# Loading q and k by tiles of all heads, and turning the last batch's q and k in the DMA path, in a fused attention and gated-convolution kernel

## The chip, the cores and the metric

The kernel runs on one core of a Trainium2 chip. The metric is device time in microseconds (us) of one execution. The core has five queues of instructions, each of which runs its own in order: PE (matrix products, with weight loads shown apart as PEld), DVE (vector), ACT (scalar), POOL (GpSimd) and SP (which here only issues transfers). Transfers run on 16 DMA engines. POOL's loads (the software queue) can change float32 to float16 on the way; SP's (the hardware queue) can't.

## What is computed

Four batches, eight heads, 768 positions, 64 numbers per head. First an attention in which each position sees the 95 positions before it, itself, and the first 8 positions of the sequence, with a bias that grows with distance by a slope of each head; then a gated convolution over the sequence on the joined heads (512 columns).

```python
scores = scale * q @ k.T                       # per batch and head, 768 x 768
keep = (pos_k < 8) | ((0 <= rel) & (rel < 96))  # rel = pos_q - pos_k
scores = where(keep, scores - slope[h] * dist, -1e9)
x = softmax(scores) @ v                        # heads joined: (4, 768, 512)
x1, x2, x3 = split(x @ w_proj)                 # 3 x 512 columns
conv = irfft(rfft(x2) * rfft(filter))          # circular, along the sequence
out = (x1 * conv * x3) @ w_out
```

## The kernel before

**Tiles.** Keys are cut into seven tiles: 120 local keys each (`KL`, starts in `K0`; the last overlaps the sixth) below the 8 global ones. A key tile meets a window of at most 216 queries (`EW`). The seven tiles form three groups, `GRP = (0,1), (2,3), (4,5,6)`; the eight heads form four pairs, and a head pair's 128 numbers fill the partitions of `QT` and `KT`, the turned q and k. Both are there once, as are `qn` and `kn`, the float16 rows before turning, and `E`, the exponentials; `vn` is there twice.

**A batch's attention** (`attention`, L849). For each head pair `turned` (L623) turns q and k on PE (six 128 x 128 transposes into one PSUM bank, L629) and ACT or DVE copies the bank out: one copy for q (L632), three for k (L635: five sixths of the tiles, the last tile, the 8 global columns for all seven). Then per group and head pair `scores` (L645: products L663, the exponential on ACT L674, the mask on DVE L691); `values` (L694: products L709 and L714, reciprocal and scaling L738, L733 or L737), `transpose_x` (L743), `gate` (L822: x1 and x3, products L832, L838, L846), and `butterfly` (L761), which folds the sequence for the short transforms. In batch 0 the bias enters by a product (L657) instead of the mask.

**A batch's convolution** (`conv`, L876): the projection of x2 (L890), its spectrum (L999), products with the filter's spectrum, the inverse (L914, L917), `mixed` and `gated` on DVE, then the output product (L946), its copy (L311) and the store on SP (L952).

**Loads.** In batch 0 q and k of head pairs 0 and 1 (`PLAIN`) come through SP as float32 into borrowed buffers (`h1`, `h2`, `pp`) and are cast by DVE (`load_pair`, L339). All else comes through POOL: q and k one head at a time (768 rows of 256 bytes, L344), v by tiles of 120 rows of all heads (960 rows, L329), weights, and the filter. `distances` (L507) makes the table of distances on POOL (L516 to L523: two iotas and four selections) and a second table (L539).

**What sets the order.** `graph` (L1084) lists the operations with their numbers. `ORDER` (L41) is one list, written out, of these numbers, each with the engine that runs it (P, A, V, G, S) and the PSUM banks that it takes; words such as `i3b6` are three dummy products on PE. Each engine's queue holds its part of this list in that order; semaphores are set only where data demand it. `bias`, costs and `after` served the making of the list; `after` also holds the list to that order, and sets no semaphore by itself.

Of the kernel before, what the change touches and what calls it, by code (L numbers as in the profile page):

```python
# [17 lines left out]
P = 128  # L18
NG = 8
KL = P - NG  # L20
# [21 lines left out]
0V 1V 2A 49S 11V 3G 5V 4V 7G 9V i3b6 17P0 46V 44A 18A 12P1 19V 55G 51S 56G 20V 43A 54G 13A 45A 42A 50V 22P2  # L42
47A 38V 14V 15V 23A 32S 52V 10V 41V 16A 53G 77G 24V 36G 90P3 39G i1b6 92P1 61S 60G i3b6 96P0 59G 48V 25V 58G
57G 30V 91A 67G 33V i4b6 86P2 93A 37V 65G 62A 21A 40V 94P1 26A 66G 104P45 87A 97V 34S 122P23 78A 63V 95V
106P01 29V 105A 68G 6V 35V 107A 156P67 88P4 8V 157A 31V 69G 89V 123A 124P01 120P45 70G 214V 215V 71G 102P67
100P2 121A 74G 158P45 216V 103A 125A 249G 98P3 101V 154P67 159A 99V 64S 235G 155A 108P23 126P45 110P67 217V
250G 160P01 218V 109A 127A 219V 111V 220V 112V 238G 161A 247G 75G 248G 115P23 128P45 133P67 227P0 113P1 116V
72G 83A 117V 134V 85A 129V 241G 225P2 237G 135V 118P3 162P67 130V 167P45 73G 114V 131P1 27A 228A 226A 81A 28V
80A 206P2 163V 223P0 164V 132A 168V 136P1 236G 165P6 240G 169V 221P7 119V 166V 84A 170P3 189V 245G 246G 137A
209V 82A 242G 224A 79A 146P6 150P1 152A 171V 229P45 239G 352P3 151P1 222A 188V 244G 243G 197V 213A 211A 76G  # L50
191V 353A 350P7 147P0 251G 231V 180P5 148V 184P3 198V 351A 153V 230A 149V 385P01 199V 190V 182A 363P67 200V
207V 476G 201V 386A 475G 364A 142P4 138P5 186A 340P0 259G 254G 338P1 232P67 212A 341A 192V 144V 193V 202V 233A
194V 387V 339V 143P3 210A 203V 185P4 140A 176P6 256G 252S 354P01 208A 145V 423P23 234A 187V 178V 196V 414P45
355A 415A 255G 344P7 342P6 195V 139P0 348P1 345V 257G 343V 424A 356V 365V 204V 141V 181P7 474G 349A 379P23
473G 357P45 346P6 347V 461G 462G 258G 472G 172P1 183V 177P0 358A 484G 376P45 417P67 380A 359V 174A 360P23 205V
179V 377A 274P1 425V 261P0 253S 418A 361A 381V 420P67 382P45 416V 362V 265P2 421A 383A 469G 275A 263P3 471G
264A 371P45 378V 419V 422V 366P67 384V 289P1 372V 367V 262A 173P3 373V 466G 287P0 266A 388P45 368V 175V 290A
389V 288A 291V 374P2 269P6 267P7 369P3 375A 270A 268A 278P0 276P2 370A 463G 279A 577P3 393P01 390V 277A 280P2
292V 578A 271V 575P7 272V 470G 394V 576A 426P45 273V 465G 281A 282P3 477G 283A 391P6 395V 431P01 396P7 392A
397A 701G 427V 588P23 480G 428V 301P4 432V 285V 433V 589A 429P5 468G 464G 284V 410P7 430A 467G 573P6 434P0  # L60
482G 610P23 406P5 302A 571P4 706G 590V 574A 611A 305P6 699G 435V 306A 286V 695G 297P0 298A 303P1 412A 572V
295P2 453V 293P4 299P3 452V 296A 307P6 481G 308A 694G 294A 304A 300V 485G 563P0 398P7 698G 402P6 585P23 408A
400A 455V 567P1 404A 310V 309V 607P45 407P7 586A 691G 454V 686G 311V 564A 568A 608A 403P6 569P2 411P3 405V
570A 440P6 399P1 456V 565P0 442A 312V 457V 582P45 409V 696G 478S 609V 458V 401V 566A 645P67 646A 693G 583A
436P2 459V 413V 499P0 639P67 640A 486P1 313V 692G 500A 479S 437P3 697G 460V 314V 438A 487A 587V 601P67 604P45
501P2 690G 483G 439V 444P3 315V 612V 602A 687G 605A 579P67 647V 648P01 709G 446A 502A 603V 448P4 642P23 580A
643A 584V 606V 688G 445P5 794P6 618P23 649A 641V 792P7 795A 447V 596P01 793A 644V 581V 597V 700G 450A 619V
503P5 504A 796P6 788P7 598V 613P01 620V 316V 591P23 800P5 614V 260G 689G 514P4 789A 449P7 797A 507P6 592V 615V
651P01 515A 801A 508A 593V 505P2 650V 317V 867P45 318V 506A 594P3 798P6 451V 868A 490P2 799A 595A 656P45 319V
657V 652V 802P7 488P6 491A 658V 803A 616P2 441P3 599P7 659P4 489A 617A 621P6 510V 492P5 653V 509V 600A 512P2  # L70
622A 443V 493A 511V 654P7 494P0 513A 320P6 495A 635P5 707G 321A 813P01 329P2 516V 496V 655A 660A 702G 870P67
869V 814A 637A 330A 636P4 517V 335P0 807P23 677V 638V 678V 871A 497V 808A 832P45 673P1 679V 790P6 520P7 680V
703S 627P2 833A 681V 532P3 704S 521A 632P7 815V 675A 873P45 631P1 533A 682V 791A 332P6 498V 874A 526P3 524P4
708G 629A 705G 633A 522P2 527A 525A 333A 518P1 674P5 834V 683V 875V 685V 336A 322S 523A 628P4 710G 530P6 531A
528P0 676V 684V 634V 519A 630V 323P5 835P23 809V 810P67 529A 804P01 726P4 324A 811A 836A 864P67 711P5 623P2
805A 535V 334S 331S 865A 534V 812V 715P3 536V 826P67 829P01 625A 712A 806V 537V 716A 713P5 830A 821P23 827A
837V 538V 872V 326P0 816P67 727A 737P4 539V 714A 822V 540V 823V 724P1 817V 327A 543V 818A 669P0 866V 541V
843P23 844V 738A 671A 828V 725A 728P5 717P4 729A 730P6 845V 665P7 718A 731A 831V 542V 719P1 739P0 624P5 720A
838P23 626V 740A 667A 670P6 325S 839V 840A 732P0 881P45 722V 672V 544V 876P67 733A 741V 819P1 661P2 662P0 877V
882V 878V 820A 721V 337S 560P1 883A 879P3 824P6 663A 735V 666P7 723V 884P4 548P2 825A 841P6 846P5 885A 742V  # L80
668V 734V 880A 664V 755P4 842A 736V 847A 747P3 557P7 756A 753P6 757P0 902V 751P4 328S 748A 903V 743P3 754A
749P5 758A 752A 905V 750A 745P6 746A 848P0 904V 744A 759V 545P4 852P3 554P6 906V 854A 911P3 546A 924P4 912A
760V 907V 551P3 549A 937P2 925A 850A 761V 908V 762V 849P4 939P0 909V 938A 910V 763V 561A 913P2 547S 851V 555A
764V 562S 940A 558A 914A 857P1 928P0 929A 917P2 915P7 918A 926P0 916A 919P2 927A 941V 920A 853P7 552A 765V
942V 930P0 932P6 766V 860P2 931A 768V 767V 550S 933A 922V 856P3 770P0 921V 858A 935V 553S 556S 923V 934V 773P3
771A 943P0 962P6 862A 774A 947P2 944A 948A 855V 936V 861P4 769V 963A 958P0 945P5 949P2 959A 964P3 863V 946A
950A 960P6 772S 776P0 779P2 965A 961A 859V 775S 777A 951V 952V 780A 967V 966V 953V 968V 785P6 954V 782P7 969V
559S 955V 890P2 898P3 970V 956V 778S 900A 971V 781S 887P0 957V 972V 894P1 886P3 973V 783A 892A 975V 974V 786A
976V 988V 896V 899P2 986V 977P6 978A 895P7 888A 983P1 897V 984A 784S 901V 787S 891P7 889V 980P6 981A 893V 979S
989V 985S 987V 999P6 993P7 1000A 982S 994A 1001S 995S 996P6 997V 990P0 998S 991A 992S  # L90
# [108 lines left out]
class Fused:  # L199
# [7 lines left out]
    LATE = frozenset(())  # L207
# [27 lines left out]
    def buffers(self):  # L235
# [5 lines left out]
        self.qn = t("qn", [P, 4, 6, 2, D])  # L241
        self.kn = t("kn", [P, 4, 6, 2, D])
# [32 lines left out]
        self.under = [[("h", 0), ("h", 2)], [("h", 1), ("h", 3)]] + [[(x, i) for x in ("p1", "p2") for i in range(2)]] * 2  # L275
        self.y = t("y", [P, 4, S])
# [43 lines left out]
    def load(self, eng, dst, src, w, nbytes, name, r=()):  # L320
        self.loads += 1
        e = {"G": self.nc.gpsimd, "S": self.nc.sync}[eng]
        return self.g.op(eng, 0.57 + 0.00035 * nbytes[0] if eng == "G" else 0.5, lambda _: e.dma_start(dst, src),  # L323
                         w=w, r=r, nbytes=nbytes, name=name, bias=-2000.0 + self.loads)
# [8 lines left out]
    def load_run(self, what, dst, src, t, n):  # L333

        rows = src[0, :, self.K0[t]:self.K0[t] + KL * n, :].rearrange("h (t p) d -> p t h d", t=n)
        self.load("G", dst[NG:P, t:t + n, :, 0:self.D], rows, [what + (i,) for i in range(t, t + n)],
                  (8 * KL * n, 256), f"load{what}{t}")

    def load_pair(self, b, hp):  # L339
        for i, (what, x, dst) in enumerate((("q", self.q, self.qn), ("k", self.k, self.kn))):  # L340
            to = dst[:, hp]
            if b or hp not in self.PLAIN:
                for hh in range(2):
                    self.load("G", to[:, :, hh], x[b, 2 * hp + hh].rearrange("(t p) d -> p t d", p=P),  # L344
                              [(what + "n", hp, hh)], (768, 256), f"{what}{hp}")
# [3 lines left out]
            self.load("S", st, x[b, 2 * hp:2 * hp + 2].rearrange("h (t p) d -> p (h t) d", p=P),  # L349
                      own[0:1], (1536, 256), f"{what}{hp}")  # L350
            st = st.rearrange("p (h t) d -> p t h d", h=2)
# [16 lines left out]
    def load_w(self, o, n):  # L368
        wr = self.w_proj.rearrange("(t p) n -> p t n", p=P)
        self.load("G", self.w[:, :, o:o + n], wr[:, :, o:o + n],  # L370
                  [("w", i) for i in range(o // P, (o + n) // P)], (512, 4 * n), f"w{o}")
# [791 lines left out]
```

## Time and profile before

| what | us |
|---|---|
| median of 3 runs (lowest, highest) | 172.21 (170.92, 172.63) |
| the profiled execution, as timed | 171.85 |
| its span in the profile | 170.1 |
| POOL's last load issue ends | 87.0 |
| turning of q and k on PE, first and last start | 5.3, 102.1 |
| score products (L663), first and last start | 12.2, 114.2 |
| first store to the output issued by SP | 97.8 |
| last product on PE ends | 166.3 |

The span begins with the first instruction and ends with the last; 1.75 us of the timed execution lie outside it. Busy times of matrix products are modelled, since they overlap one another, so a PE that is busy throughout need not run at its peak. "Landing" is the time from the issue of a transfer to the first sign that it arrived. The order's 1006 words stand for 1002 operations and 4 groups of dummy products.

### The profile page before, as it was taken

To read this page: it belongs to the slowest core of one execution; us is meant where nothing else is said; L and a number is where in the kernel's file an instruction comes from. 1 tells how busy PE (TensorE), PEld (TensorE's weight loads), DVE (VectorE), ACT (ScalarE), POOL (GpSimd) and SP (SyncE) were. 2 spreads that over 40 slices of the span, in tenths; PEclk is the share of its full clock that TensorE was granted. 3 is DMA by queue.
4 is the path that set the end of the run, shared out by engine and by line. 5 is a ranking of instruction groups with operands and counts; after the bars stand their busy time and mean duration, and the time that the engine had idled before them with its cause. 6 is when DMAs were issued, how large, how long until landed. Compare 5 with 4: busy or idle time off the path is not lost. (4 is left out here: it accounts for less than half of the span.)

```text
span 170.1 us, 4259 instructions
## 1 busy us (share of the span) xinstructions
PE 160.6 (94%) x1614; PEld 96.2 (57%) x1614; DVE 155.9 (92%) x364; ACT 150.2 (88%) x308; POOL 81.9 (48%) x107
## 2 busy tenths in 40 slices
PE   7795998999999999999999999999999999999981
PEld 2452347766655688555677546646577644565540
DVE  5993789999999999999999999999999999999950
ACT  5779499999999999999999999999999789894441
POOL 8997999999799899999940000000000000000000
PEclk9999599999999999999999999999999999999999
DMA  6999999999999999999999110330100013343344
GB/s 133 194 200 190 154 158 166 176 160 161 157 158 136 130 111 135 121 133 112 135 148 91 14 62 4 123 123 14 51 2 4 0 62 123 129 185 123 149 186 158
DMA packets 87139, 20.30 MB, mean 119 GB/s; under 512 B 79872, under 2 KB 84176, under 8 KB 87120
## 3 DMA queue, kind: packets, MB, share of 16 engines
q0 software_dynamic: 76976, 11.84, 95.5%
q1 hardware_dynamic: 10144, 8.20, 15.6%
q8 instruction: 12, 0.20, 0.5%
q14 instruction: 7, 0.06, 0.1%
HBM read 25.25 MB, written 6.29 MB: 185 GB/s over the span
## 5 line engine op out<-in xcount | busy, mean ns | idle before, releaser
L832 PE MATMUL bank<-xT,w 128*128 128x384 f16 x256 | 49.1, 326 | 0.0
L674 ACT ACTIVATE E<-bank 128x864 f16<-128x864 f32 x48 | 41.8, 952 | 2.5 <-PE bank L663 2.5
L832 PEld LDWEIGHTS <-w 128*128 128x128 f16 x256 | 23.5, 98 | 16.3 <-issue 1.1
L323 POOL DMA_DIRECT2D vn<-in_v_dram x28 | 26.1, 959 | 2.5 <-DMA g<-in_moe_filter_fft_dram 1.4
L323 POOL DMA_DIRECT2D kn<-in_k_dram x28 | 24.0, 869 | 0.8 <-PE bank L629 0.7
L946 PE MATMUL bank<-wo,y 128*128 128x512 f16 (+1 forms) x100 | 23.7, 370 | 0.7 <-DVE y L995 0.7
L323 POOL DMA_DIRECT2D qn<-in_q_dram x28 | 23.8, 864 | 0.3 <-PE bank L917 0.2
L691 DVE TENSOR_TENSOR E<-E,mask 128x864 f16<-128x864 f16 x36 | 20.4, 595 | 0.0
L311 ACT ACTIVATE ot<-bank 128x512 f32<-128x512 f32 (+1 forms) x24 | 14.9, 636 | 5.4 <-PE bank L946 4.8
L311 ACT ACTIVATE x<-bank 128x384 f16<-128x384 f32 x28 | 15.8, 590 | 3.6 <-PE bank L832 3.4
L846 DVE TENSOR_TENSOR g<-bank,x 128x384 f16<-128x384 f32 x32 | 17.0, 547 | 0.5 <-ACT X L307 0.3
L733 DVE TENSOR_TENSOR xn<-bank,rc 128x512 f16<-128x512 f32 (+1 forms) x21 | 15.9, 771 | 0.1
L890 PE MATMUL bank<-w,xs 128*128 128x512 f16 x64 | 16.0, 379 | 0.0
L709 PE MATMUL bank<-vn,E 128*128 128x65 f16 x224 | 15.2, 193 | 0.7 <-DVE xn L733 0.5
L663 PE MATMUL bank<-QT,KT 64*128 64x216 f16 (+2 forms) x224 | 15.6, 248 | 0.0
L714 PE MATMUL bank<-vn,E 128*128 128x65 f16 x192 | 15.0, 193 | 0.0
L946 PEld LDWEIGHTS <-y 128*128 128x128 f16 x100 | 9.5, 98 | 9.6 <-DVE y L995 1.2
L709 PEld LDWEIGHTS <-E 128*128 128x128 f16 x224 | 13.9, 97 | 1.5 <-issue 0.3
L307 ACT CAST X<-bank 128x512 f16<-128x512 f32 x24 | 14.7, 732 | 0.0
L663 PEld LDWEIGHTS <-KT 64*128 64x128 f16 x224 | 7.8, 95 | 12.0 <-issue 10.8
L714 PEld LDWEIGHTS <-E 128*128 128x128 f16 x192 | 13.2, 97 | 1.7 <-issue 1.1
L307 ACT COPY KT<-bank 128x720 f16<-128x720 f16 (+2 forms) x36 | 13.6, 524 | 0.2 <-PE bank L629 0.2
(156 smaller groups left out, 343.6 us busy)
## 6 DMA issues: line engine op xcount, KB each, us to landing
out_dram<-ot SPq DMA_DIRECT2D x23, 256.0 KB, 2.0
vn<-in_v_dram POOLq DMA_DIRECT2D x28, 120.0 KB, 6.3
kn<-in_k_dram POOLq DMA_DIRECT2D x28, 96.0 KB, 5.2
qn<-in_q_dram POOLq DMA_DIRECT2D x28, 96.0 KB, 4.9
w<-in_moe_w_proj_dram POOLq DMA_DIRECT2D x4, 256.0 KB, 6.4
g<-in_moe_filter_fft_dram POOLq DMA_DIRECT2D x1, 768.0 KB, 11.3
w<-in_moe_w_proj_dram POOLq DMA_DIRECT2D x1, 512.0 KB, 7.4
wo<-in_moe_w_out_dram POOLq DMA_DIRECT2D x1, 512.0 KB, 8.1
```

Of the source, the lines that this page charges most:

```text
L307: {"A": nc.scalar.copy, "V": nc.vector.tensor_copy, "G": nc.gpsimd.tensor_copy}[e](out, in_)
L311: self.nc.scalar.mul(out, in_, c)
L323: return self.g.op(eng, 0.57 + 0.00035 * nbytes[0] if eng == "G" else 0.5, lambda _: e.dma_start(dst, src), w=w, r=r, nbytes=nbytes, name= ...
L663: nc.tensor.matmul(bs[hh].f32()[:, off:off + w], self.KT[hs, hp, P * m:P * m + P], self.QT[hs, hp, KL * m:KL * m + w], start=(off == 0 and ...
L674: g.op("A", act(864), lambda _: nc.scalar.activation(eo, bs[0].two()[:, :, 0:432].rearrange("p h (m w) -> p h m w", m=2), Act.Exp, scale=s ...
L691: g.op("V", dve(864, 2), lambda _: nc.vector.tensor_mul(eo, eo, mk), r=[("mask", 2 * hp), ("mask", 2 * hp + 1)], w=[("E", hp, gi)], name=" ...
L709: nc.tensor.matmul(o[:, n, hh], ef[:, at:at + P], vt[:, t, 2 * hp + hh, 0:D + 1], start=first, stop=(t == 0), skip_group_check=True)
L714: nc.tensor.matmul(o[:, n, hh], ef[:, at:at + P], vt[:, t - 1, 2 * hp + hh, 0:D + 1], start=False, stop=True, skip_group_check=True)
L832: nc.tensor.matmul(bk.f32()[:, 0:h], self.w[:, c, o + P * j:o + P * j + P], self.xT[:, c, h * s:h * s + h], start=(c == 0), stop=(c == 3))
L846: g.op("V", dve(h, 1, True), lambda _: nc.vector.tensor_mul(x3, pts[1].f32()[:, 0:h], x1), use=[pts[1]], r=[key], w=[ko], name="g")
L890: nc.tensor.matmul(bk.f32(), src[:, c], w[:, c, DM:2 * DM], start=(c == 0), stop=(c == 3))
L946: nc.tensor.matmul(bk.f32()[:, 0:n], y[:, c, P * t:P * t + P], self.wo[:, c, cs], start=(c == 0), stop=(c == 3))
```

## The change

Four things change, and `ORDER` is a new list of 994 words (990 operations, 4 groups of dummy products).

- **q and k of batches 1 to 3 by tiles.** `qn` and `kn` lie by tile, `[P, 6, 512]` and `[P, 7, 512]`. `load_tiles` replaces eight loads each of 768 rows by six each of 128 rows of all heads (1024 packets). The six transposes of a head pair read all six tiles; a tile can be overwritten when all four head pairs are turned.
- **The last batch (`CROSS = (3,)`) is not turned on PE.** Its keys are loaded as seven tiles of 120 rows, the 8 global rows are copied within SBUF into the first partitions (two transfers on SP), and `cross` issues 13 transposing transfers on SP, each turning a tile `[128 rows, 512]` into `[128, 4, 128]` of `KT` or `QT`. The 8 operations of `turned` and their 8 copies go. The score products of that batch wait for tiles of `KT` and `QT` instead of head pairs.
- **POOL's start.** The first table of distances stands ahead of POOL's first loads.
- **The order.** The engines of the copies that ACT or DVE can make are chosen anew, too. In the new list SP's first loads are k of pair 1, q of pair 0, v's first rows, q of pair 1, k of pair 0 (before: q1, k1, q0, v's first rows, k0), and POOL's are the filter, then single heads of k and q of pairs 2 and 3.

The counts of operations by engine in the two lists, where they differ:

| operation | before | after |
|---|---|---|
| loads of q, k, v by POOL | 84 | 73 |
| turns on PE | 32 | 24 |
| copies of turned q: ACT, DVE | 10, 6 | 5, 7 |
| copies of turned k: ACT, DVE | 12, 4 | 8, 4 |
| scaling of values (two tiles): ACT, DVE | 2, 14 | 6, 10 |
| copies of turned x (two tiles): ACT, DVE | 14, 2 | 10, 6 |
| same, three tiles: ACT, DVE | 5, 3 | 6, 2 |
| casts of batch 0's q, k: ACT, DVE | 0, 4 | 3, 1 |
| copies of x1: ACT, DVE | 28, 4 | 30, 2 |
| outputs: ACT, DVE | 24, 1 | 21, 4 |
| scaling of the projection: ACT, DVE | 24, 0 | 22, 2 |
| transposing transfers on SP | 0 | 13 |

```diff
-    LATE = frozenset(())
+    CROSS = (3,)
...
-        self.qn = t("qn", [P, 4, 6, 2, D])
-        self.kn = t("kn", [P, 4, 6, 2, D])
+        self.qn = t("qn", [P, 6, DM])
+        self.kn = t("kn", [P, 7, DM])
...
+    def load_tiles(self, b):
+        sides = [("q", self.q, self.qn, P, 0, range(0, self.S, P)), ("k", self.k, self.kn, P, 0, range(0, self.S, P))]
+        if b in self.CROSS:
+            sides[1] = ("k", self.k, self.kn, KL, NG, self.K0)
+        for n in range(7):
+            for what, x, dst, rows, low, starts in sides:
+                if n < len(starts):
+                    lo = starts[n]
+                    self.load("G", dst[low:P, n].rearrange("p (h d) -> p h d", h=self.H),
+                              x[b, :, lo:lo + rows, :].rearrange("h p d -> p h d"),
+                              [(what + "n", n, h) for h in range(8)], (8 * rows, 256), f"{what}{n}")
+            if n == 0 and b in self.CROSS:
+                for lo, hi in ((0, 2), (2, 7)):
+                    self.load("S", self.kn[0:NG, lo:hi], self.kn[NG:2 * NG, 0:1].to_broadcast([NG, hi - lo, self.DM]),
+                              [("kg", lo)], (8 * (hi - lo), 1024), "vglobal", r=[("kn", 0, h) for h in range(8)],
+                              after=self.turns)
+
+    def cross(self):
...
+                out = dst[:, :, P * n:P * n + P]
+                self.g.op("S", 1.3, lambda _, out=out, src=src, n=n: nc.sync.dma_start_transpose(out, src[:, n]),
...
+                          w=[(what + "T", n)], nbytes=(128, 1024), name="xbar",
+                          after=loads + [x for gi in gis for x in self.before[gi]])
...
-                nc.tensor.transpose(b.f16()[:, P * t:P * t + P], buf[:, hp, t].rearrange("p h d -> p (h d)"), self.ident)
+                nc.tensor.transpose(b.f16()[:, P * t:P * t + P], buf[:, t, P * hp:P * hp + P], self.ident)
...
+        src = [("QT", hp), ("KT", hp)]
+        if self.b in self.CROSS:
+            src = [("kT", m) for m in m0] + [("qT", n) for n in range(KL * m0[0] // P, (
+                KL * m0[-1] + self.EW[m0[-1]] - 1) // P + 1)]
...
-            if c == 0:
+            if c == 0 and b in self.CROSS:
+                self.cross()
+            elif c == 0:
...
+        self.distances()
         for i in range(4):
-            self.load_pair(0, i)
-            if i == 0:
-                self.distances()
+            self.load_pair(i)
...
-        for i in range(4):
-            self.load_pair(b, i)
+        self.load_tiles(b)
```

More of the change, by code (lines that the diff above doesn't have):

```diff
@@ L47 @@
[L47 to L51, printed above, removed]
@@ L317, in evac, with load @@
         return {"A": act(n), "V": dve(n, psum=True)}
-    def load(self, eng, dst, src, w, nbytes, name, r=()):
+    def load(self, eng, dst, src, w, nbytes, name, r=(), after=()):
         self.loads += 1
@@ L323, in load @@
         return self.g.op(eng, 0.57 + 0.00035 * nbytes[0] if eng == "G" else 0.5, lambda _: e.dma_start(dst, src),
-                         w=w, r=r, nbytes=nbytes, name=name, bias=-2000.0 + self.loads)
+                         w=w, r=r, nbytes=nbytes, name=name, after=after, bias=-2000.0 + self.loads)
     def load_rows(self, what, dst, src, b, t):
@@ L352, in load_pair @@
             self.g.op("AV", {"A": act(768), "V": dve(768, 2)}, lambda e, to=to, st=st: self.copy(e, to, st),
-                      r=own, w=[(what + "n", hp, 0), (what + "n", hp, 1)], name="cast")
+                      r=own, w=keys[0] + keys[1], name="cast")
+    def load_tiles(self, b):
[14 more added lines that the diff above has]
+                              after=self.turns)
@@ new lines, in cross @@
+    def cross(self):
+        nc, S = self.nc, self.S
+        loads = [x for x in self.g.ops if "G" in x.cost and x.bytes]
+        for n in range(7):
+            for what, src, dst, ok in (("k", self.kn, self.KT, True), ("q", self.qn, self.QT, n < 6)):
+                if not ok:
+                    continue
+                gis = [gi for gi, ms in enumerate(self.GRP) if (n in ms if what == "k" else any(
+                    KL * m < P * n + P and KL * m + self.EW[m] > P * n for m in ms))]
+                out = dst[:, :, P * n:P * n + P]
+                self.g.op("S", 1.3, lambda _, out=out, src=src, n=n: nc.sync.dma_start_transpose(out, src[:, n]),
+                          r=[(what + "n", n, h) for h in range(8)] + ([("kg", 0 if n < 2 else 2)] if what == "k" else []),
+                          w=[(what + "T", n)], nbytes=(128, 1024), name="xbar",
+                          after=loads + [x for gi in gis for x in self.before[gi]])
@@ L370, in load_w @@
         self.load("G", self.w[:, :, o:o + n], wr[:, :, o:o + n],
-                  [("w", i) for i in range(o // P, (o + n) // P)], (512, 4 * n), f"w{o}")
+                  [("w", i) for i in range(o // P, (o + n) // P)], (512, 4 * n), f"w{o}", after=self.ahead)
     def setup(self):
@@ L628, in turn @@
             for t in range(6):
-                nc.tensor.transpose(b.f16()[:, P * t:P * t + P], buf[:, hp, t].rearrange("p h d -> p (h d)"), self.ident)
-        g.op("P", pe(*[P] * 6), turn, acq=[b], r=["ident", (what + "n", hp, 0), (what + "n", hp, 1)], name=what)
+                nc.tensor.transpose(b.f16()[:, P * t:P * t + P], buf[:, t, P * hp:P * hp + P], self.ident)
+        self.turns.append(g.op("P", pe(*[P] * 6), turn, acq=[b], r=["ident"] + [
+            (what + "n", t, 2 * hp + hh) for t in range(6) for hh in range(2)], name=what))
         if what == "q":
@@ L1063, in load_first @@
         self.load("G", self.fl, self.filt.rearrange("(t p) n -> p t n", p=P),
-                  [("g", 1, j, s) for j in range(4) for s in range(2)], (768, 2048), "filter")
+                  [("g", 1, j, s) for j in range(4) for s in range(2)], (768, 2048), "filter", after=self.ahead)
     def first_rows(self, vt):
```

118 lines of the change are left out of this document (64 added, 54 removed).

## The prediction

> **What bounds the kernel now.** I read the busy times first, then the stretches of time, then the by-shape groups of the operations that go, then the start on DVE, SP and POOL.
>
> ```profile
> PE 160.6 (94%) x1614; PEld 96.2 (57%) x1614; DVE 155.9 (92%) x364; ACT 150.2 (88%) x308; POOL 81.9 (48%) x107
> ```
>
> Three engines are nearly full. The stretches (columns: length, then busy time of PE, PEld, DVE, ACT, POOL, the granted clock, DMA share, GB/s) say where they aren't:
>
> ```profile
> 15.00:20.00 5.00, 3.25 (x20) 1.04 (x20) 3.86 (x11) 3.18 (x5) 3.55 (x5) 0.75 2.26 160
> 30.00:40.00 10.00, 10.00 (x110) 6.70 (x106) 9.78 (x26) 9.67 (x20) 9.75 (x13) 1.00 2.06 163
> 100.00:110.00 10.00, 10.00 (x100) 6.29 (x98) 9.97 (x21) 10.00 (x23) 0.00 (x0) 1.00 0.14 52
> 150.00:160.00 10.00, 10.00 (x70) 5.83 (x69) 10.00 (x30) 5.96 (x15) 0.00 (x0) 1.00 0.46 176
> ```
>
> From 30 to 160 us PE and DVE run at 98% or more, ACT nearly so until 130. What is idle lies at the start (DVE 6.3 us, ACT 6.4 us in the first 30) and in the last 8 us. So the time can fall in two ways: less work on all three engines, or an earlier filling. What goes is shown by the by-shape groups (busy us, mean ns, idle before):
>
> ```profile
> L307 ACT COPY KT<-bank 128x720 f16<-128x720 f16 x12 | 10.3, 857 | 0.2 <-PE bank L629 0.2
> L629 PE MATMUL bank<-ident,kn 128*128 128x128 f16 x96 | 8.8, 233 | 2.5 <-DVE kn L307 2.5
> L307 ACT COPY QT<-bank 128x768 f16<-128x768 f16 x10 | 8.5, 906 | 0.4 <-PE bank L629 0.4
> ```
>
> The start, from the timelines of DVE and SP (start, length, operation, idle before it and what ended that):
>
> ```profile
> 16.00 0.56 DVE L307 CAST kn<-h 128x768 f16<-128x768 f32 x1 [2.25 <-DMA h<-in_k_dram]
> 5.41 0.39 SPq L323 DMA_DIRECT2D h<-in_k_dram  x1
> ```
>
> The fifth SP load, k of pair 0, is issued at 5.41 and arrives at 16.0. PE waits 1.7 us for it, ACT then 1.8, and the clock in the stretch falls to 0.75. In the window 3 to 5 us, with POOL's packets not yet there, SP's queue had the DMA engines to itself:
>
> ```profile
> q1 hardware_dynamic: 1943, 0.49, 130.3%
> q0 software_dynamic: 21, 0.00, 2.1%
> ```
>
> That is 1.03 ns a packet; later, mixed with POOL's packets, it moved 0.36 MB in 4 us.
>
> **The change, part by part.** *Turns on PE.* 48 of 192 transposes go. Six of them take 0.50 us in PE's timeline and one alone 0.22, so their pitch is 0.057 us: 48 x 0.057 = 2.7 us. They lie among PE's full stretches, so it counts if PE is the one that ends last.
>
> *Copies on ACT and DVE.* By the two orders' letters and the rows' busy time over count: on ACT four k copies of 1.57 (10.3 + 4.5 + 4.0 over 12) and five q copies of 0.85 go, 10.5 us; with four two-tile x copies of 0.63, three outputs of 0.63 and two projections of 0.72, 16.3. Back come four scalings of values (eight small activations of 0.24 each, 7.7 us), three casts of some 0.85, two x1 of 0.56 and 0.8 of single ones, 12.1. Net -4.2 us. On DVE scalings (4 x 0.66), casts (3 x 0.59), x1 (2 x 0.55) and single ones (1.7) go, 7.2; x copies (4 x 0.40), outputs (3 x 0.68), projections (2 x 0.68), a q copy and small ones (1.2) come, 6.2. Net -1.0 us.
> With all three engines full the saving is at least DVE's 1.0, if DVE ends last everywhere, and at most PE's 2.7. I take 1.9, the middle, since waits between 30 and 160 us change sides too often for one engine to own them.
>
> *POOL's first loads behind the distances.* The table takes 2.3 us (6.44 to 8.78) and now stands before the loads, which start at about 4.4 instead of 2.06; the same set of issues is done by about 13 us either way. The packets of the first POOL load came 3 us after its issue, so SP has the engines alone until about 7.3: from 1.85 us at 0.25 to 0.28 MB/us, its 1.59 MB are through by 8 to 9. So k of pair 0 comes at about 9 instead of 16. Upper end of the gain: DVE's 2.25 us and 1.2 behind it, 3.4. Lower end: what comes next. The new PE queue turns all four k of batch 1, does four x1 gates and turns q before it goes on, and with tiles a turn needs the last of six loads.
>
> *Tile loads.* 768 packets take POOL 0.87 us, 960 take 0.96, so 0.48 ns more a row and 0.99 for 1024. Twelve of these are 11.9 against 16 x 0.87 = 13.9: 2.0 us less for batches 1 and 2 each, 1.2 for batch 3, whose seven k tiles carry 576 packets more. POOL is idle after 87 us, so by itself this is worth nothing; it brings the last load to about 80, landing (5 to 6 us) by 86. But q of batch 1 is now complete only when POOL, past batch 0's v at 20.8 as before, has issued 12 tiles and a weight load: 20.8 + 12.7 = 33.5, and 5.2 to land, 38.7. PE was at its first gate at 33.2; four k turns (1.4), a filter product (0.4) and four gates (2.8) bring it to 37.8, less what the start gained. It would wait for whatever is gained beyond -0.9. So the start is worth between -0.9 and 3.4; I take 0.5, near the lower end, since this wait is counted from rows and the engines behind it have work left.
>
> *The crossbar.* 13 transfers on SP, of 128 KB each, and two small copies. No row shows a transposing transfer. Below: q's load at 1.03 ns per 256 bytes is 0.53 us for 512 such packets. Next: SP spaced its loads of 384 KB by 1.6 to 1.7 us. Above: if the crossbar works in 32-byte pieces, 4096 x 1.03 = 4.2 us. I take 1.5, near the spacing row, as that is the same queue under load. The sources: the turns of batch 2 free `qn` at about 66 us (by the place in the order: products of batch 2's scores ran from 62 to 82); 14 loads of about 0.96 later POOL is at 80, q lands by 85. The score products of batch 3 stand in the new order where the old one was at 103 to 116 us; the last group needs all 13 tiles at about 113. Twelve after 85 with 2 us to land may take (113 - 85 - 2) / 12 = 2.2 us each; the first group's five have more. So at 1.5 it is hidden with 8 us to spare. Behind it on SP wait the stores, first due at 97.8 before; six output buffers cover them. If the cover is gone, PE, ACT and DVE wait in order: PE's queue holds the projections of batch 2 behind those products.
>
> A rule speaks against this part. The Trainium skill (VectorE: DVE Perf Modes, "The three transpose paths") gives 1309 ns for one 128 x 128 turn in the DMA crossbar against 390 on TensorE, and says to use TensorE where PSUM will do. Here PE's pitch is 57 ns, far below that page's figure; whether its 1309 holds for each of the four squares of a transfer no run shows. By an estimate from it, four in a row make 5.2 us a transfer, and the sum would be some 205 us; from rows this is the first rival.
>
> *Sum.* -1.9 - 0.5 = -2.4 us on 171.85; the median is 0.36 above the profiled run, so 172.2 - 2.4 = 169.8. Best case, -2.7 - 3.4: 166.1.
>
> **Rivals.** *Slow crossbar, slower.* It decides from 2.2 us a transfer. At 3 us: 85 + 36 + 2 = 123 against 113, ten late: 169.8 + 10 = 180. At 4.2: 85 + 50 + 2 = 137: 194. For it: nothing in the trace bounds the piece size. Against: the loads are over by then, and the DMA share is 0.14 between 100 and 110 us. Chance 0.19.
> *Late tiles.* Turns wait for the slowest of six loads, in batch 1 as above and again in batch 2, whose q tiles are reissued only after all four q turns. The start's gain is lost (-0.9) and 0.5 to 1 us goes at batch 2: 172.2 - 1.9 + 0.9 + 0.8 = 172.0, up to 175 if both engines behind run dry. For it: POOL is 98% busy from 30 to 80, so a tile can't be pulled in. Against: DVE and ACT have other work queued. Chance 0.29, of which 0.05 over 1% slower.
> *Not behind all loads.* `after` sets no semaphore, so transposes could run beside the last loads, as k of pair 0 did at 10.6 us. But the second transposing transfer needs the last q tile but one, so only one overlaps; it costs nothing and belongs to the forecast.
>
> **How the numbers follow.** A measurement of this kernel can tell about 1% (170.5 to 173.9) from no change. Forecast, 166.1 to 170.4: 0.52. Late tiles: 0.24 within 1%, 0.05 above. Slow crossbar: 0.19. So faster 0.52, same 0.24, slower 0.24. The range for 8 in 10 runs from 166.1 to 177, which leaves out the slow crossbar above 2.7 us a transfer (0.15) and a little below.
>
> **What would show it.** Right: the cast of k of pair 0 before 11 us, no fall of the clock before 20; PE's turns 144; the transposing transfers spaced under 2.2 us and over before 110; ACT's busy time about 146, DVE's 155. Wrong: PE idle before L663 with a DMA as releaser near 105 to 115 (slow crossbar), or before L629 with a DMA of `qn` near 37 or 60 (late tiles).

## The result, and the profile after

| | before | after |
|---|---|---|
| median, us (lowest to highest, runs) | 172.42 (170.92 to 173.99, 4) | 177.84 (177.40 to 178.95, 4) |
| profiled execution, us; its span | 171.85; 170.1 | 178.95; 177.2 |
| first exponential (L674, now L713) | 14.4 | 23.7 |
| first gate product (L832, now L871) | 33.2 | 44.3 |
| last exponential | 115.4 | 126.8 |
| last output product (L946, now L990) | 165.9 | 173.1 |

The ratio is 1.035, with a 95% interval of 1.026 to 1.045: 3.5% slower. Here and below, medians and ranges have all executions of a kernel, while ratios leave out those that took over 1.5% longer than its fastest. The table of moments (starts in the two traces) already says where: the changed kernel is 9.3 us behind at its first exponential, 11.4 behind at its last, and 7.2 behind at its last product. The loss is at the start, and the later part wins some 4 us of it back.

The page's busy times and granted clock of the changed kernel:

```profile
PE 161.4 (91%) x1574; PEld 95.1 (54%) x1574; DVE 153.3 (87%) x364; ACT 151.5 (86%) x322; POOL 74.6 (42%) x96
...
PEclk9995589999999999999999999999999999999999
```

DVE and POOL have less to do. PE's busy time is no lower, since part of its work ran at half clock (in filter_late below, at full clock throughout, it is 159.0), and the new list has 19 dummy products where the old one had 11. The same four stretches as before (length, busy time of PE, PEld, DVE, ACT, POOL, clock, DMA share, GB/s):

```profile
15.00:20.00 5.00, 2.23 (x15) 1.69 (x16) 1.02 (x4) 2.81 (x6) 3.58 (x4) 0.50 2.30 157
30.00:40.00 10.00, 9.65 (x162) 6.01 (x161) 8.23 (x20) 9.94 (x13) 10.00 (x13) 1.00 1.86 128
100.00:110.00 10.00, 10.00 (x98) 6.92 (x97) 10.00 (x20) 10.00 (x28) 0.00 (x0) 1.00 0.55 94
150.00:160.00 10.00, 10.00 (x75) 5.88 (x75) 10.00 (x19) 9.31 (x20) 0.00 (x0) 1.00 0.28 105
```

Between 15 and 20 us DVE works 1.0 us of five (3.9 before) and PE at a clock of 0.50 (0.75 before). The stretch at 100 is as full as it was, although the crossbar now works there. Turns and copies by shape (busy us, mean ns, idle before):

```profile
L307 ACT COPY KT<-bank 128x720 f16<-128x720 f16 x8 | 6.8, 852 | 0.0
L663 PE MATMUL bank<-ident,kn 128*128 128x128 f16 x72 | 6.3, 234 | 7.9 <-ACT kn L307 6.6 <-DVE eo L563 1.3
L307 ACT COPY QT<-bank 128x768 f16<-128x768 f16 x5 | 4.2, 843 | 0.3 <-PE bank L663 0.3
```

The counts are those that the list of operations promised; what is new is the idle time in front of a k turn, 6.6 us behind one cast. The timelines of ACT, PE, SP and POOL (start, length, operation, idle before it and what ended that) lead to it:

```profile
10.91 0.83 ACT L307 CAST qn<-pp 128x768 f16<-128x768 f32 x1 [3.49 <-DMA pp<-in_q_dram]
16.88 0.83 ACT L307 CAST kn<-h 128x768 f16<-128x768 f32 x1 [4.00 <-DMA h<-in_k_dram]
17.77 0.82 PE L663 MATMUL bank<-ident,kn 128*128 128x128 f16 x6 [6.61 <-ACT kn L307]
4.07 1.73 SPq L323 DMA_DIRECT2D h<-in_k_dram  x1
3.92 0.96 POOL L323 DMA_DIRECT2D g<-in_moe_filter_fft_dram  x1
```

SP issues k of pair 0 earlier than before (4.07 against 5.41), and it arrives later (16.9 against 16.0); q of pair 1, SP's fourth load, is late as well. PE has nothing else: the turn of k of pair 0 stands in front of every score product in the new list. At 3.92 us POOL issued the filter. The DMA queues from 8 to 12 us (packets, MB, share of 16 engines):

```profile
q0 software_dynamic: 714, 0.64, 102.8%
q1 hardware_dynamic: 375, 0.10, 17.9%
```

POOL's queue (q0) moves 0.64 MB and SP's (q1) 0.10; before, SP's moved 0.36 MB in the same window. SP had moved 1.19 of its 1.59 MB by 8 us. The missing 0.40, one load, took until 16.

### The profile page after: what moved, and what is told of

The parts are those of the page before. It is cut to its first block, busy times and chain, and to the rows that moved or that the text cites. A ratio compares the mean times of both kernels' runs of the same rounds, so it can differ in the third digit from the quotient of the medians.

```text
span 177.2 us, 4199 instructions
## 1 busy us (share of the span) xinstructions
PE 161.4 (91%) x1574; PEld 95.1 (54%) x1574; DVE 153.3 (87%) x364; ACT 151.5 (86%) x322; POOL 74.6 (42%) x96
## 3 DMA queue, kind: packets, MB, share of 16 engines
q1 hardware_dynamic: 17288, 9.97, 21.5%
## 4 chain that ended last, share of the span: by engine, by line
ACT 44%; PE 38%; DMA 7%; issue 4%; DVE 3%; SPq 2%; DVEq 0%; ACTq 0%
ACT E L713 15%; PE bank L871 9%; PE bank L990 9%; DMA h<-in_k_dram 7%; PE bank L934 6%; ACT xn L776 6%; ACT x L311 4%; ACT eo L307 3%; ACT X L307 3%; ACT ab L311 3%; PE bank L663 2%; ACT mask L587 2%; ACT xT L307 2%; SPq L323 2%; PE bank L698 2%
## 5 line engine op out<-in xcount | busy, mean ns | idle before, releaser
L871 PE MATMUL bank<-xT,w 128*128 128x384 f16 x256 | 49.2, 326 | 0.3 <-DVE x L313 0.3
L713 ACT ACTIVATE E<-bank 128x864 f16<-128x864 f32 x48 | 41.5, 950 | 1.8 <-PE bank L698 1.6
L871 PEld LDWEIGHTS <-w 128*128 128x128 f16 x256 | 23.4, 97 | 15.3 <-issue 1.5
L323 POOL DMA_DIRECT2D kn<-in_k_dram x23 | 20.8, 907 | 12.3 <-ACT eo L311 6.7
L990 PE MATMUL bank<-wo,y 128*128 128x512 f16 (+1 forms) x100 | 22.7, 370 | 0.0
L323 POOL DMA_DIRECT2D qn<-in_q_dram x22 | 19.6, 907 | 3.2 <-DMA wo<-in_moe_w_out_dram 1.6
L311 ACT ACTIVATE x<-bank 128x384 f16<-128x384 f32 x30 | 16.6, 574 | 1.9 <-PE bank L871 1.8
L311 ACT ACTIVATE ot<-bank 128x512 f32<-128x512 f32 x21 | 13.1, 650 | 5.3 <-PE bank L990 2.6
L990 PEld LDWEIGHTS <-y 128*128 128x128 f16 x100 | 9.5, 97 | 9.4 <-DVE y L1039 0.2
L307 ACT CAST eo<-bank 128x384 f16<-128x384 f32 x32 | 14.4, 534 | 0.1
L776 ACT ACTIVATE xn<-bank,rc 128x64 f16<-128x64 f32 x60 | 14.0, 538 | 0.0
```

Of the source, the lines that this page charges most:

```text
L307: {"A": nc.scalar.copy, "V": nc.vector.tensor_copy, "G": nc.gpsimd.tensor_copy}[e](out, in_)
L311: self.nc.scalar.mul(out, in_, c)
L713: g.op("A", act(864), lambda _: nc.scalar.activation(eo, bs[0].two()[:, :, 0:432].rearrange("p h (m w) -> p h m w", m=2), Act.Exp, scale=s ...
L776: nc.scalar.mul(to[:, i, n], o[:, i, n, 0:D], rc[:, i, n])
L871: nc.tensor.matmul(bk.f32()[:, 0:h], self.w[:, c, o + P * j:o + P * j + P], self.xT[:, c, h * s:h * s + h], start=(c == 0), stop=(c == 3))
L990: nc.tensor.matmul(bk.f32()[:, 0:n], y[:, c, P * t:P * t + P], self.wo[:, c, cs], start=(c == 0), stop=(c == 3))
```

## The experiments

Thirteen kernels were run, in four groups, each group beside runs of the kernel before on its chip. Edits of the order are shown in its words: the number of an operation, its engine, its PSUM banks.

### Where the start is lost

**One step of the kernel before, moved.** GpSimd's load of the filter (77G) goes ahead of two single-head loads of q, to the time that it has in the changed kernel; nothing else is touched.

```diff
-... 55G 51S 56G 20V 43A 54G ... 53G 77G 24V 36G ...
+... 55G 51S 56G 20V 43A 77G 54G ... 53G 24V 36G ...
```

> The kernel before with one step moved: GpSimd issues the filter's load ahead of the last two single-head loads of q instead of behind them, at about 3.9 us as in the changed kernel (5.6 before). Nothing else is changed. Theory (the filter's 2 KB packets take the engines from SyncE's queue, whatever the order of the rest): from 8 to 12 us SyncE's queue moves 0.1 to 0.25 MB instead of 0.36; q of pair 0, its third load, is cast at 11 to 14 us instead of 9.1, the first scores stand behind its turn on PE, first exponential 15.5 to 18 instead of 14.4, total 1 to 4 us slower (ratio 1.005 to 1.025). Rival (the filter's place costs nothing by itself, and only the new order of PE and ScalarE made it cost): first exponential within 0.7 us of 14.4, ratio 0.995 to 1.004.

Measured: 176.68 us (176.31 to 177.33), ratio 1.033 [1.027, 1.039]: slower by more than the theory's range, and nearly as slow as the whole change (1.035). Its DMA queues from 8 to 12 us, then POOL, PE and ACT:

```profile
q0 software_dynamic: 931, 0.69, 110.6%
q1 hardware_dynamic: 410, 0.10, 19.4%
```

```profile
3.87 0.84 POOL L322 DMA_DIRECT2D g<-in_moe_filter_fft_dram  x1
4.67 1.69 POOL L322 DMA_DIRECT2D qn<-in_q_dram  x2
...
16.81 0.80 PE L628 MATMUL bank<-ident,qn 128*128 128x128 f16 x6 [4.54 <-DMA qn<-in_q_dram]
...
18.84 0.89 ACT L673 ACTIVATE E<-bank 128x864 f16<-128x864 f32 x1 [3.34 <-PE bank L662]
```

SP's queue falls to 0.10 MB as in the changed kernel. But the theory named the wrong victim: q of pair 0, SP's third load, was cast at 9.05 as before. PE waited 4.5 us for a head of q that POOL itself had queued behind the filter. Here the large load was felt by what stood behind it in its own queue, in the changed kernel by what shared the engines with it; which of the two a kernel feels depends on its list. First exponential 18.84 instead of 14.4.

**The filter later, in the changed kernel.** Its load goes behind GpSimd's eight single-head loads, and the four sums on DVE that read it go behind the copies of batch 0's turns.

```diff
-... 93A 77G 39A ... 79A 25V 54G 96P6 ...
+... 93A 39A ... 79A 25V 54G 77G 96P6 ...
```

> The changed kernel with the filter's load behind the eight single-head loads of POOL, and DVE's first four sums on the filter behind its copies of batch 0's turns; SP's order and PE's stay. If the filter's 2 KB packets starve SP's queue (0.10 MB in the 4 us from 8 to 12): q of pair 1 by 8, k of pair 0 by 11, first exponential at 15 to 17, and 171 to 174. If SP's queue is starved by any POOL packets: k of pair 0 still at 15 to 17, and 176 to 179.

Measured: 171.66 us (170.83 to 175.84, 10 runs), ratio 1.001 [0.998, 1.005]. DMA queues from 8 to 12 us, then ACT:

```profile
q0 software_dynamic: 2131, 0.27, 106.9%
q1 hardware_dynamic: 1471, 0.42, 58.3%
```

```profile
8.41 0.83 ACT L307 CAST qn<-pp 128x768 f16<-128x768 f32 x1 [0.98 <-DMA pp<-in_q_dram]
...
10.73 0.83 ACT L307 CAST kn<-h 128x768 f16<-128x768 f32 x1 [0.35 <-DMA h<-in_k_dram]
```

With GpSimd's small packets beside it, SP's queue moves 0.42 MB and k of pair 0 is there at 10.7. No clock falls, and the whole 3.5% is gone.

**The other way round.** The filter stays where the change put it; SP's loads are put in the order q1, k1, q0, v's first rows, k0, and the turn of k of pair 0 goes behind score products of pair 1, its cast to DVE; the casts and the turn of q of pair 1 move forward.

```diff
-... 51S 45S 6V 61S 49S 31V 13A 47S ... 88P0 ... 56G 105A 8V 156P01 157A 120P67 ...
+... 49S 51S 45S 6V 61S 47S 31V 13A ... 56G 105A 8V 48V 156P01 88P3 89V 157A 120P67 ...
```

> The changed kernel with SP's first loads in the old order (q1, k1, q0, v's first rows, k0) and the turn of k of pair 0 behind the three score products of pair 1; the filter still leads POOL's loads. If the first scores' place behind the fifth SP load costs the time: first exponential at 13 to 15 and 170 to 173. If what counts is that k of pair 0 comes at 16.9 at all (ACT dry behind it), only 2 to 4 us come back: 174 to 176. If the start is covered: 177 to 179.

Measured: 172.41 us (171.89 to 174.11), ratio 1.007 [1.001, 1.013]; first exponential at 16.5. K of pair 0 was cast at 15.5 (16.9 in the changed kernel), and that costs little when nothing stands behind it. So the changed kernel's loss needs both: the filter in front, and a PE list that can't begin without the load that it delays.

**The old start, whole.** The first 114 steps are those of the kernel before, the rest is the new list; the table of distances no longer has to stand ahead of POOL's loads.

```diff
-ORDER: the new list
+ORDER: the first 114 words of the old list, then the new list without what they hold
```

> The changed kernel with the first 114 operations of the old order (its first loads on SP and POOL, its distances behind POOL's first loads, its batch 0 turns and first scores), and the new order for all the rest: tile loads and the crossbar stay. Theory A, the loss is made in the first 25 us (first exponential at 23.7 instead of 14.4) and passes through: first exponential at 14 to 15, time 167 to 171, below both kernels by what the crossbar saves. Rival B, the tile loads make the loss (POOL stands still from 21.9 to 28.5 until batch 0's k is turned, batch 1's turns come late): 174 to 178. Rival C, the crossbar or its waits make it: 176 to 178.

Measured: 175.25 us (173.70 to 176.19), ratio 1.018 [1.009, 1.028]. The time lies in rival B's range, but the run does not say what it was made for. Four tables of masks that the old list has late and the new one early fell between ACT's exponentials, and PE waited for them:

```profile
29.17 0.88 PE L693 MATMUL bank<-eo 128*128 128x432 bf16 x2 [3.17 <-ACT E L714]
```

A seam between two lists is a new list, and its first loss is at the seam.

### ACT's tables

The new list has the last sine of the filter's folding behind the first exponentials, so ACT loads its tables twice more (start, length):

```profile
35.53 1.28 ACT L474 ACT_TABLE_LOAD   x1
...
37.48 1.28 ACT L587 ACT_TABLE_LOAD   x1
```

The Trainium skill (ScalarE: Activation LUTs, "What ACT_TABLE_LOAD costs") gives 1283 ns and a drain of 1380 ns for a switch. The first number agrees; no drain is seen here, as the sine begins 0.02 us after the load and the masks 0.01 us.

**The sine early**: its two vector steps and the sine move ahead of the exponentials.

```diff
-... 46V 38A 20V i3b6 86P3 ... 37V 36V 21A 60G ... 27V 24V 83A ... 216V 25V 54G ... 159A 26A 115P01 ...
+... 46V 38A 20V 24V 25V i3b6 86P3 ... 37V 36V 21A 26A 60G ... 27V 83A ... 216V 54G ... 159A 115P01 ...
```

> The changed kernel with the third sine (L474) and its two sums ahead of the first exponential, so that ACT does not load its tables twice more at 35.5 and 37.5 us (2.56 us). If ACT owns the stretch behind the late start: 175 to 176. If the stretch waits for loads or PE: within 0.8 of the changed kernel, 177 to 178.6.

Measured: 176.40 us (175.05 to 176.69), ratio 1.024 [1.016, 1.033], 1.4 us below the changed kernel and between the two expected ranges; the interval overlaps that of the changed kernel. In its profiled execution, the fastest of four, the first exponential came at 21.2 instead of 23.7, ahead of the place of the two loads. So the 1.4 us can't be put down to them.

**Both** (the later filter and the early sine):

> Filter's load behind the eight single heads, and the third sine ahead of the exponentials: both repairs of the start in one kernel; tiles and crossbar stay as in the change. If the late k of pair 0 and ACT's two table loads are all that the change lost: 168 to 170.5, ratio to the old kernel 0.975 to 0.99. If the table loads are hidden once the start is early: 171 to 172, ratio about 1.00.

Measured: 172.07 us (171.45 to 174.17), ratio 1.006 [1.000, 1.011]. On top of the repaired start the early sine brings nothing that can be told; ACT's busy time is 148.8; from 30 to 40 us it falls from 9.97 us in filter_late to 6.97, and the first gate starts at 37.3 as against 37.2. What the two loads took turns up as idle time.

**All three repairs** (pair 1 first as well, and the cast of v's first rows later):

> The run filter_sine with SP's first loads in the old order, the turn of k of pair 0 behind pair 1's three products, and the cast of v's first rows later on ACT. If the first scores' wait for the fifth SP load still costs with the filter out of the way: first exponential at 12.5 to 14 instead of 15.4, and 1 to 2 us below filter_sine. If batch 0 then waits for its next loads instead: within 0.5 of it.

Measured: 172.21 us (170.68 to 174.72), ratio 1.004 [1.000, 1.008]. One repair of the start is enough, and none makes the changed kernel faster than the one before.

### Crossbar and tiles

**No crossbar** (from the kernel with the later filter and the early sine): the last batch is turned on PE again, its 8 turns and copies put by hand where their data are there, between words 550 and 640 of the list.

```diff
-    CROSS = (3,)
+    CROSS = ()
```

> The run filter_sine with the last batch turned on PE again: eight turns and eight copies (four on ACT, four on DVE), six tiles of 128 keys, no transposing transfer. By the prediction's sum (PE 2.7 us, and here ACT 4.8 and DVE 2.9 more): 2 to 4 us above filter_sine. If the crossbar's saving was given back in waits: within 0.7 of it. If the crossbar costs: below it.

Measured: 178.02 us (177.30 to 178.82), ratio 1.039 [1.032, 1.046], 6 us more than with the crossbar, and more than the 2 to 4 that were expected. PE's busy time is 3.8 us higher, ACT's 4.0, DVE's 3.6. The 6 us are an upper estimate of the crossbar's worth: DVE worked 7.5 us of the ten from 100 to 110, so the places chosen by hand cost some of it.

**Batches 1 and 2 by heads** (from the same kernel), sixteen loads in the places of the twelve:

```diff
+    def load_heads(self, b):
+        for hp in range(4):
+            for what, x, dst in (("q", self.q, self.qn), ("k", self.k, self.kn)):
+                for hh in range(2):
+                    h = 2 * hp + hh
+                    self.load("G", dst[:, 0:6, 64 * h:64 * h + 64], x[b, h].rearrange("(t p) d -> p t d", p=P), ...
-        self.load_tiles(b)
+        (self.load_tiles if b in self.CROSS else self.load_heads)(b)
```

> The run filter_sine with q and k of batches 1 and 2 loaded one head at a time in the order of their turns (16 loads for 12 tiles); batch 3 by tiles for the crossbar. If a turn's wait for the last of six tiles, and a tile's wait for all four turns, cost time (the late tiles of the prediction): 1 to 3 us below filter_sine. If POOL's time is what counts (2 us more a batch): 0.5 to 2 above. If neither: within 0.5.

Measured: 173.30 us (172.52 to 173.47), ratio 1.011 [1.005, 1.016], 1.2 us more than with tiles. POOL's busy time rises from 74.9 to 79.8. This points to tiles as the better loads with the new start; the interval overlaps that of filter_sine, so it is not shown.

**The old start again, with a cleaner seam.** 187 steps of the old list, through batch 0's attention; batch 1's tiles in the places of its old loads; then the new list.

```diff
-ORDER: the new list
+ORDER: the first 187 words of the old list (tiles of batch 1 for its heads), then the new list without what they hold
```

> The first 187 steps of the old order (start, batch 0's attention up to its first gates; first loads, filter and distances in their old places), with batch 1's q and k loaded by tiles in the old loads' places, then the new order for all that is left (tiles and crossbar as in the changed kernel). Theory (the loss lies wholly in the start; tiles and crossbar gain as far as they are not eaten up there): first exponential 14 to 15 us, first gate 33 to 36, total 166.5 to 169.5 us, ratio to the kernel before 0.965 to 0.985, so faster than both. Rival (the later stages of the new order win nothing by themselves; what the repaired kernels make up after the start is only slack that a late start leaves): first gate 33 to 36 all the same, total 171 to 174, ratio 0.995 to 1.01. If the seam stalls, a PE idle time of over 2 us shows between 30 and 40 us.

Measured: 171.96 us (171.52 to 173.43, 10 runs), ratio 1.006 [1.002, 1.011]; first exponential 15.3, first gate 36.8. By the time the theory falls and its rival stands, but PE's timeline shows a cause that neither named:

```profile
35.72 0.51 PE L664 MATMUL bank<-ident,kn 128*128 128x128 f16 x6 [2.23 <-DMA kn<-in_k_dram]
...
41.33 1.12 PE L664 MATMUL bank<-ident,qn 128*128 128x128 f16 x17 [1.01 <-DMA qn<-in_q_dram]
```

The turns of batch 1 wait for tiles, 3.2 us together: the prediction's second rival, at 36 to 41 us. Neither the changed kernel nor filter_late shows it. In filter_late POOL has issued the last k tile at nearly the same time (29.3 us, 29.6 here), but PE comes to the first turn of batch 1 at 36.1 and not, as here, at 33.5.

With only 133 old steps, up to the first value products:

```diff
-ORDER: the new list
+ORDER: the first 133 words of the old list (tiles of batch 1 for its heads), then the new list without what they hold
```

> As hybrid_188, but only the first 133 steps are the old ones: start, scores and exponentials of batch 0; the value products, the folding of the filter and the gates follow the new order. Theory (loss before the first exponentials): first exponential 14 to 15 us, first gate 35 to 38, total 168 to 171. Rival (the new order's value and filter stage of batch 0 is what loses the 4 us between first exponential and first gate that the repaired kernels show): first gate 37 to 39 and a total of 171 to 173, while hybrid_188 is 2 us or more below it.

Measured: 172.91 us (171.15 to 174.40, 4 runs), ratio 1.013 [1.005, 1.022]; first gate at 36.3, no later than in hybrid_188. The interval overlaps that of hybrid_188, so this run tells little.

**Tiles first** in GpSimd's queue, the projection weights (72G, 73G, 75G) behind them; GpSimd's words in their order:

```diff
-74G 240G 244G 238G 239G 75G 242G 72G 246G 236G 73G 243G 235G 245G 241G 237G 76G
+74G 240G 244G 238G 242G 246G 236G 239G 243G 235G 245G 241G 237G 75G 72G 73G 76G
```

> hybrid_188 with GpSimd's queue alone changed: batch 1's six k tiles, then its six q tiles, all ahead of the three column blocks of projection weights that stood between them (the weights come right behind, by 36 us; the first projection is at 51). In hybrid_188 the first turn of batch 1 waited 2.23 us for a k tile at 35.7 and a q turn 1.01 us at 41.3. Theory (with the old start the tiles are late, since a turn needs all six tiles of its batch, and that ate what the new order's later stages win): both waits go, PE's idle time from 20 to 60 us falls from 4.3 to 1 to 2 us, total 168.5 to 170.5, ratio 0.98 to 0.995. Rival (PE's idle time there is slack that turns up again at the next wait): the two waits go, total 171 to 173, ratio 0.998 to 1.01.

Measured: 175.10 us (173.65 to 177.52), ratio 1.013 [1.007, 1.019]. Both waits went, and a worse one came:

```profile
39.57 4.02 PE L872 MATMUL bank<-xT,w 128*128 128x384 f16 x12 [3.37 <-DMA w<-in_moe_w_proj_dram]
```

The expectation had the weights needed at the projection, 51 us. The gates read them first (`bank<-xT,w`), at 36. It was an error about this kernel, and the run says nothing about tiles.

**Batch 1 by heads, batches 2 and 3 as changed**, on hybrid_188:

```diff
+    HEADS = (1,)
-        self.load_tiles(b)
+        (self.load_heads if b in self.HEADS else self.load_tiles)(b)
```

> hybrid_188 with batch 1's q and k loaded by single heads, as in the kernel before (16 loads in place of 12, pairs in the order of the new turns); batches 2 and 3 by tiles, batch 3 turned by the crossbar. A turn of batch 1 then needs four loads, not all of them. Theory of late tiles: the 2.23 us wait goes, the q turns wait 0 to 2 us since 16 loads cost GpSimd 3.6 us more, total 169 to 171. Rival (slack, as above): 171 to 173.5.

Measured: 171.26 us (170.04 to 172.62, 12 runs) against 172.72 (171.10 to 174.16, 17 runs), ratio 0.992 [0.989, 0.995]: of thirteen versions the one that is faster than both kernels, by 0.8%, less than the 1% that the prediction called the least that can be told. The time lies just inside the range of the rival (171 to 173.5). The page's busy times, and two stretches:

```profile
PE 158.2 (93%) x1566; PEld 93.5 (55%) x1566; DVE 155.2 (92%) x365; ACT 148.6 (88%) x319; POOL 77.4 (46%) x100
```

```profile
20.00:40.00 20.00, 17.79 (x246) 11.38 (x246) 17.67 (x45) 18.38 (x31) 19.05 (x24) 0.98 2.06 158
40.00:60.00 20.00, 19.81 (x224) 11.71 (x223) 19.68 (x47) 19.82 (x38) 17.40 (x20) 1.00 2.24 162
```

No turn waits for a load of batch 1. PE idles 2.4 us from 20 to 60 (4.3 in hybrid_188, 0.6 before), so not all of its 2.4 us less work (160.6 to 158.2) reaches the end: the median is 1.5 us below that of the kernel before. Where the gain over hybrid_188 lies is not shown: the two ran on different chips, and in the trace shown here k of pair 0 came later (PE worked 2.6 us from 15 to 20, 4.0 in hybrid_188) and the first gate at 37.4, not 36.8.

## Why the prediction was wrong

**What bounds the kernel** was read rightly, and so was the place to look: a kernel full from 30 to 160 us can only lose or win at its start, or by less work.

**The step that failed** is *POOL's first loads behind the distances*: "so SP has the engines alone until about 7.3: from 1.85 us at 0.25 to 0.28 MB/us, its 1.59 MB are through by 8 to 9. So k of pair 0 comes at about 9 instead of 16." The first half holds in the main: POOL's packets came at about 6.7 us and SP's queue had moved 1.19 MB by 8. In the second half, the step's own rates leave 0.06 to 0.23 MB at 7.3 us (0.40 were left at 8), and it took them as good as through: it asked only when POOL's first packets come, not which. They were the filter's, which the text on the change names as POOL's first load. The bounds for the start, -0.9 to 3.4 us, held no loss from the load order; it was -9.3 at the first exponential. The trace of before had the warning, in its DMA queues from 12 to 16 us, with the filter under way:

```profile
q0 software_dynamic: 1158, 0.67, 117.1%
q1 hardware_dynamic: 335, 0.13, 18.6%
```

SP's queue moved 0.13 MB, and that is when k of pair 0 was late there. filter_late shows that the loss goes when the filter moves. filter_early_before shows what the filter's place costs by itself, there through POOL's own queue. No run moved the distances alone.

The same step read the new PE queue only from batch 1 on. That every score product stands behind k of pair 0 was in the list; pair1_first, which moves SP's loads and the casts as well, shows what the order is worth while the filter is in front, some 5 us.

**Turns on PE**, -2.7 us predicted: hybrid_heads1, with the dummy products of the kernel before and nearly its clock (0.74 from 15 to 20 us, 0.75 before), has 158.2 us against 160.6, so -2.4; no_crossbar and filter_sine, both at full clock, differ by 3.8. Right in size; how much of it reaches the end no run shows by itself.

**Copies**: ACT was to lose 4.2 us. Without the two table loads (2.6 us) it lost 1.3; 148.9 against 150.2. The letters of the list don't show where the activation function changes, and four scalings cost what was counted (14.0 against 6.7 us) while the copies of turned x that left ACT were its short ones. DVE was to lose 1.0 and lost 2.6. The net of 1.9 us for three engines was never seen: the repaired kernels tie.

**Tile loads**: 2.0 us less of POOL per batch was right in sign (heads_12: 4.9 us for two batches). The bound from POOL's count, "38.7" against PE's 37.8, pointed to the right place: with the old start, hybrid_188 waits for q tiles until 41.3, and until 35.7 for a k tile, the longer wait, which the bound did not count. It did not matter in the changed kernel, whose first gate came 11 us late, nor in filter_late. But "past batch 0's v at 20.8 as before" failed with the start: POOL had to wait 6.7 us for the turns of batch 0 and began at 28.5 us.

**The crossbar**, 1.5 us a transfer against a break-even of 2.2: SP's timeline after (first and last of thirteen transfers)

```profile
96.78 1.31 SPq L384 DMA_TRANSPOSE KT<-kn  x1
...
113.65 2.58 SPq L384 DMA_TRANSPOSE KT<-kn  x2
```

shows the first and the last of them; most held SP's queue for 1.2 to 1.3 us, one for 1.84, and no engine waited for one. Hidden, as forecast. The first rival (3 to 4.2 us) is refuted; so is 5.2 by an estimate from the Trainium skill's 1309 ns a square (VectorE: DVE Perf Modes, "The three transpose paths"): SP's queue took four squares in the time that it gives for one, and all thirteen transfers were issued within 19.5 us.

**Signs named in advance**: k of pair 0 before 11 us, no clock fall before 20, ACT near 146 (151.5) and transfers over before 110 all failed, the first two by the filter's place (in filter_late the cast is at 10.7 and the clock stays full), the last since the start was late (in filter_sine the last transfer is issued at 107.6); DVE's 155 came to 153.3; PE's 144 transposes, the spacing under 2.2 us (but for the first gap, 2.6), and no PE wait before score products at 105 to 115 came true. What would show the failed step was named, but the rival on the slower side was looked for in the crossbar, the operation that no row priced. The loss came from a load that a row had priced, moved by 1.7 us.

**Still open**: what the crossbar alone is worth (the 6 us of no_crossbar have the hand-placed turns in them, the 1.5 of hybrid_heads1 the tiles of batches 2 and 3 and a new list), and why the kernels with a repaired start reach their first gate 4 us later than the kernel before (filter_late 37.2, filter_sine 37.3, against 33.2), a loss that they only make up by the end. Part of it is the list, which puts k turns before the gates. Another part may come with the repair itself, by PE's and POOL's timelines of filter_late:

```profile
23.93 0.22 PE L748 MATMUL bank<-vn,E 128*128 128x65 f16 x2 [1.35 <-DMA vn<-in_v_dram]
22.56 0.91 POOL L323 DMA_DIRECT2D vn<-in_v_dram  x1 [1.45 <-DMA g<-in_moe_filter_fft_dram]
```

The filter, now later, is under way when v is loaded: PE waits for v and works 3.1 us of the five from 20 to 25 (5.0 before).

## What to carry to other kernels

Read the first loads of every queue in the new list by size, not by count: a large load with long packets takes the engines from another queue's short ones for as long as it lasts, and holds up all that is behind it in its own. Then ask which first product waits for what it delays. A repaired stall uncovers the next one (here loads of v in filter_late, tiles in hybrid_188): look for it in the trace before calling the rest of the change worthless.

## What the runs showed of the hardware

- Two queues that both had packets waiting were mostly served packet for packet, whatever the size. From 10 to 15 us in filter_early_before POOL's queue moved 1326 packets and SP's 1330, from 10 to 14 us in the changed kernel 1138 and 1121; in bytes, 0.56 and 0.34 MB, and 0.40 and 0.29, as the filter's packets are long. The Trainium skill says that each DMA engine goes round the queues by packets (DMA: Bandwidth & Descriptors, "Queues, rings and completion order"); these counts agree. From 8 to 10 us in the changed kernel, with the filter under way, they don't: POOL's queue moved 355 packets and SP's 48, and no run shows why.
- POOL's first packets came 2.6 to 3.1 us after the issue (3.92; the first half microsecond with any is 6.5 to 7.0).
- The granted clock fell to 0.50 from 15 to 20 us, after 6.6 us in which PE had nothing to do, was 0.66 from 20 to 25 and full from 25 on; filter_late kept 1.00 in all of them.
- Of thirteen transposing transfers of 128 KB each, twelve held SP's queue for 1.2 to 1.3 us, while PE, DVE and ACT were busy for 10.0 of 10 us (100 to 110), and no engine waited for one.
